# Block-causal attention with routed experts on one core: routing tables moved into PSUM, 64-byte list entries, a stacked tail product, and SP's queue in program order

## The chip, the cores and the metric

The kernel runs on one core of a Trainium2 chip. The metric is the device time in microseconds of one execution. The core has five engines that work through their own queues in order: PE (TensorE, matrix products; its weight loads are shown as PEld), DVE (VectorE), ACT (ScalarE), POOL (GpSimd) and SP (SyncE, which here only issues DMAs). POOL issues DMAs too, the indirect ones among them.

## The reference

What is computed, cut to its core:

```
scores = q @ k.T / 8                      # 8 batches x 8 heads, 576 positions, 64 channels
scores = where(i // 64 >= j // 64, scores, -1e9)
attn   = softmax(scores)                  # fp32, sums guarded by 1e-9
x      = (attn @ v) as rows of 512        # 4608 rows, 8 heads side by side
logits = x @ w_gate + modality_bias[modality_id]      # 8 experts
e      = argmax(logits);  gate = softmax(logits)[e]
out    = gate * (relu(x @ w1[e]) @ w2[e])             # w1: 512 x 1024, w2: 1024 x 512
```

The products must hold fp32 accuracy. The kernel gets it from products in fp32r by splitting operands into a head (the value rounded to fp32r) and a low half (value minus head) and adding head x head, head x low and low x head.

## The kernel before, in words

**Pairs and slots.** The 64 heads are taken in 32 pairs; four pairs make a batch of 576 rows. The program is written as slots. Slot s works on the front of pair s (stage 0) and on the back of pair s-1 (stage 1). What every engine does in a slot, and in which order, is one hand-written list, ORDER (L48): "SA2" are the scores of head A, row block 2; "M" the row maxima on DVE (L261); "E" the exponentials on ACT (L287); "T" the transposes on PE (L313 to L327); "C" the copies of transposed probabilities to SBUF as heads on ACT (L338); "D" their low halves on DVE (L343); "X", "Y", "W" the products with v (L380); "x", "y" the copies of their results on ACT; "K" the product that turns the result back into rows and adds the gate's columns (L399, L401); "Z" the scaling into the rows xr and the gate's sums gl on DVE (L412 to L415). "r" and "p" are the sums and reciprocals of a pair (L349 to L356). FIRST and LAST are the lists of the first and the last slot.

**Splitting q and k (split_qk, L194).** Once a slot, for the pair that follows, POOL casts the raw k (L198), subtracts to get k's low half on partitions 0 to 63 (L199), casts the raw q (L201) and subtracts to get q's low half (L202). q's raw tile holds the same 64 rows twice, so that q's head stands on partitions 0 to 63 and the low half, L202, on 64 to 127. SP copies k's low half (k2t, L192) and q's head (L204, into z) to where the second score product reads them, and loads the next q into the only raw tile (L184). Then POOL splits v (L233).

**The tail.** A head has 576 = 4 x 128 + 64 rows. Probabilities of the last 64 columns are transposed beside "TA1" (L321) and copied to a tile p4 in fp32 (L338); the product with v's last 64 rows is one fp32 product on 64 partitions at the end of "Y" (L378, L380).

**Routing.** Behind the last "Z" of a batch, routing(b) (L420) gives 24 small steps, which the places "q0" to "q7" in ORDER take one at a time (two at a time behind slot 24), and "qp", "qv" the steps for PE and what follows them. They form logits from gl (L429), treat the late 64 rows apart (L434 to L446), add the bias (L449), find the largest and the expert's number (L453 to L476), the gate's weight (L493 to L505), counts per expert by two small products (L481, L482), running sums (L500), and each row's place in its expert's list (L516 to L531). All these tables are SBUF tiles; the small products use the one bank of pool ps_b, which "K" also uses. With the weight, weight_out stores the batch's rows to DRAM (xrows, rows of 513 floats: 512 and the weight; L507 to L512, on SP). place_out appends five list writes to `placing`: indirect DMAs on POOL (L533), each of which writes 128 row numbers, four bytes each, to their places in idlist in DRAM. "vh" issues two of them per slot, behind v's split.

**SP's order.** For the first four slots (NSP, L39) SP's DMAs are issued in the order of the program; from then on a planner places them, by its own costs and due times. The four compute engines keep the program's order throughout.

**Experts.** Behind batch 5, `choose` (L565) picks the two largest experts and their first rows, weights are staged and cast during the last slots, and run_all (L934) works through tiles of 256 gathered rows: gather (L833), transposes (L846), two products (L864, L910), and an indirect store of the output rows (L913). fill (L624) sets idlist to a number that the gathers skip, before the first list write.

Of the kernel before, what the change touches and what calls it, by code (L numbers as in the profile page):

```python
# [25 lines left out]
PPB = H // 2  # L26
XW = 513
# [11 lines left out]
NSP = 4  # L39
# [52 lines left out]
def attention_moe(ctx, tc, qk, vr, bkw, mid, mb, w1, w2, cf, ci, cm, ld, out):  # L92
# [6 lines left out]
    idlist = drm.tile([NROW, 1], I32, name="idlist")  # L99
# [10 lines left out]
    idt = cst.tile([128, B, 5], I32, name="idt")  # L110
# [23 lines left out]

    q2s, k2s, zs, pts = [], [], [], []
# [17 lines left out]
    xrb = [rt.tile([128, 4, XW], F32, name=f"xr{i}", bufs=1) for i in range(2)]  # L153
    scatters, placing = [], []
# [39 lines left out]
    def split_qk(p):  # L194
        d = pairs[p]
        k = d.raw[0:64, 0:1152].rearrange("p (h c) -> p h c", h=2)
        q = rawq[64:128].rearrange("p (h c) -> p h c", h=2)
        pool.tensor_copy(d.qk[:, 1280:2560], d.raw)  # L198
        pool.tensor_tensor(d.k2[0:64], k, d.k[0:64], ALU.subtract)  # L199
        gather_low(d)  # L200
        pool.tensor_copy(d.qk[:, 0:1280], rawq)  # L201
        pool.tensor_tensor(d.q[64:128], q, d.q[64:128], ALU.subtract)  # L202
        if p > 2:
            nc.sync.dma_start(d.q2[0:64].bitcast(F32), d.q[0:64, :, 0:512].bitcast(F32))  # L204
        load_q(p + 1)

    def split_half(p, h):
# [7 lines left out]
        (dve, pool)[p * h].tensor_tensor(d.q[64:128, h], rawq[64:128, qs], d.q[64:128, h], ALU.subtract)  # L215
        act.copy(d.q2[0:64, h], d.q[0:64, h, 0:512])
# [6 lines left out]
    def load_v(p):  # L223
        d = pairs[p]
        d.vr = att.tile([128, 640], F32, name="vrt", bufs=3)
        nc.sync.dma_start(d.vr, vr[p])
        d.v = att.tile([128, 8, 2, 64], F32R, name="vhl", bufs=2)

    def split_v(p):
        d = pairs[p]  # L230
        v8 = d.vr[:, 0:512].rearrange("p (a b) -> p a b", a=8)
        act.copy(d.v[:, :, 0], v8)
        pool.tensor_tensor(d.v[:, :, 1], v8, d.v[:, :, 0], ALU.subtract)  # L233
# [58 lines left out]
    def transposes(p, u):  # L292
# [23 lines left out]
        elif u[1] == "1":  # L316
# [23 lines left out]
    def rests(p, u):  # L340
        for s, dst in pairs[p].copies[u]:
            if len(dst) > 1:
                dve.tensor_tensor(dst[1], s, dst[0], ALU.subtract)  # L343
# [14 lines left out]
    def values(p, h, part):  # L358
        d = pairs[p]
        if part == "X":  # L360
            d.o[h, 0] = ps_o.tile([128, 512], F32, name="o0")
# [32 lines left out]
    def back(p, h):  # L394
        d = pairs[p]
        d.b[h] = ps_b.tile([128, 512], F32, name="b")
# [23 lines left out]
    def routing(b):  # L420
        xr, xt, gl = xrs[b]
        g = Pair()

# [3 lines left out]
        def logits():  # L427
            g.lg = t([128, 5, NE], name="lg")
            dve.tensor_reduce(g.lg[:, 0:4], gl, AX.X, ALU.add)  # L429

        def late_logits():
            g.lt = t([128, 2, NE], name="lt")
            lt = xt.rearrange("p q c -> p c q")
            dve.tensor_reduce(g.lt[:, 0], lt[:, 0:8], AX.X, ALU.add)  # L434
            dve.tensor_reduce(g.lt[:, 1], lt[:, 72:80], AX.X, ALU.add)

        def late_half():
            dve.tensor_tensor(g.lt, g.lt, hm.unsqueeze(2).to_broadcast([128, 2, NE]), ALU.mult)
            dve.tensor_tensor(g.lt[:, 0], g.lt[:, 0], g.lt[:, 1], ALU.add)

        def late_total():
            g.tot = ps_b.tile([128, 512], F32, name="b")
            pe.matmul(g.tot[:, 0:NE], ii, g.lt[:, 0], start=True, stop=True)

        def late_copy():
            dve.tensor_copy(g.lg[:, 4, :], g.tot[:, 0:NE])  # L446

        def biased():
            dve.tensor_tensor(g.lg, g.lg, bias[:, 5 * b : 5 * b + 5, :], ALU.add)  # L449

        def top():
            g.mx = t([128, 5], name="mx")
            dve.tensor_reduce(g.mx, g.lg, AX.X, ALU.max)  # L453

        def shifted():
            g.df = t([128, 5, NE], name="df")
            dve.tensor_tensor(g.df, g.lg, bc(g.mx), ALU.subtract)
# [5 lines left out]
        def hits():  # L463
            g.eq = t([128, 5, NE], name="eq")
            dve.tensor_tensor(g.eq, g.lg, bc(g.mx), ALU.is_equal)

        def hit_index():
            dve.tensor_tensor(g.eq, g.eq, iom40, ALU.mult)

        def first():  # L470
            g.ix = t([128, 5], name="ix")
            dve.tensor_reduce(g.ix, g.eq, AX.X, ALU.min)

        def onehot():
            g.oh = t([128, 5, NE], BF16, name="oh")
            dve.tensor_tensor(g.oh, iov40, bc(g.ix), ALU.is_equal)  # L476

        def counts():
            g.ps = ps_b.tile([128, 512], F32, name="b")
            ohe = g.oh.rearrange("p c e -> p (c e)")  # L480
            pe.matmul(g.ps[:, 0:40].rearrange("p (e c) -> p c e", e=NE), ones, ohe.rearrange("p (c e) -> p c e", e=NE), start=True, stop=True)  # L481
            pe.matmul(g.ps[:, 40:80], lead, ohe, start=True, stop=True)  # L482
# [6 lines left out]
        late_copy.kind = counts_copy.kind = "qv"

        def weight():
            g.sm = t([128, 5], name="gs")
            dve.tensor_reduce(g.sm, g.ex, AX.X, ALU.add)  # L493

        def weight_guard():
            dve.tensor_scalar(g.sm, g.sm, GUARD, None, ALU.add)

        def running():
            g.cum = t([128, NE, 5], name="cum")
            dve.tensor_tensor_scan(g.cum.rearrange("p e c -> p (e c)"), first5.rearrange("p e c -> p (e c)"), g.pc[:, 0:40], 0.0, ALU.mult, ALU.add)  # L500

        def weight_out():
            g.wt = t([128, 1], name="wt")
            dve.reciprocal(xr[:, :, 512], g.sm[:, 0:4])
            dve.reciprocal(g.wt, g.sm[:, 4:5])  # L505
# [6 lines left out]
            queue.dma_start(late[:, 512:513], g.wt[64:128])  # L512

        def place():
            g.pos = t([128, 5, NE], name="pos")
            dve.tensor_tensor(g.pos, g.pc[:, 40:80].rearrange("p (c e) -> p c e", c=5), g.cum.rearrange("p e c -> p c e"), ALU.add)  # L516

        def place_run():
            dve.tensor_tensor(g.pos, g.pos, run.unsqueeze(1).to_broadcast([128, 5, NE]), ALU.add)

        def place_pick():
            dve.tensor_tensor(g.pos, g.pos, g.oh, ALU.mult)
            dve.tensor_tensor(run, run, g.cum[:, :, 4], ALU.add)

        def place_sum():
            g.pp = t([128, 5], name="pp")
            dve.tensor_reduce(g.pp, g.pos, AX.X, ALU.add)

        def place_out():
            g.pi = t([128, 5], I32, name="pi")  # L530
            dve.tensor_tensor(g.pi, g.pp, inv5, ALU.add)  # L531
            def scatter(c):
                last = pool.indirect_dma_start(idlist[:], bass.IndirectOffsetOnAxis(ap=g.pi[:, c : c + 1], axis=0), idt[:, b, c : c + 1], None, bounds_check=NROW - 1, oob_is_err=False)  # L533
# [6 lines left out]
        return [logits, late_logits, late_half, late_total, late_copy, biased, top, shifted, hits, expo, hit_index, first, onehot, weight, weight_guard, weight_out, counts, counts_copy, running, place, place_run, place_pick, place_sum, place_out]  # L540
# [3 lines left out]
    def pick(eng, val, name):  # L544
        mx = cst.tile([128, 1], F32, name=f"mx_{name}")
        kx = cst.tile([128, NE], F32, name=f"kx_{name}")
# [6 lines left out]
        eng.tensor_scalar(oh, iom8, ix, None, ALU.is_equal)  # L553
# [10 lines left out]

    def choose(eng):  # L565
        cnt, cnb, lead, rest, start = (cst.tile([128, NE], F32, name=n) for n in ("cnt", "cnb", "taken", "rest", "start"))
        eng.tensor_tensor(cnt, run, base8, ALU.subtract)
        sel["oha"], sel["ea"] = pick(eng, cnt, "a")
# [3 lines left out]
        sel["ohb"], sel["eb"] = pick(eng, cnb, "b")  # L572
        eng.tensor_tensor(rest, base8, lead, ALU.add)
        sel["ra"] = dot(eng, oha, base8, "a")
        sel["rr"] = dot(eng, oha, rest, "r")
        sel["rb"] = dot(eng, sel["ohb"], base8, "b")
        eng.scalar_tensor_tensor(start, oha, float(COVER - LEAD), rest, ALU.mult, ALU.add)
        eng.scalar_tensor_tensor(start, sel["ohb"], float(COVER_B), start, ALU.mult, ALU.add)
# [55 lines left out]
    def prepare_bias(dst, r):  # L634
# [10 lines left out]
        prepare_fill,  # L645
    ]

# [430 lines left out]
```

## Time and profile before

| what | value |
|---|---|
| median of three timed runs | 934.86 us (934.0 to 944.07) |
| the profiled execution's own time | 926.34 us |
| its span, first to last instruction | 924.2 us |
| mean granted TensorE clock | 0.962 |
| PE busy | 862.1 us, 93% |
| DVE busy | 506.8 us, 55% |
| ACT busy | 456.3 us, 49% |
| POOL busy | 442.8 us, 48% |
| DMA moved | 116.44 MB, mean 126 GB/s |

All profile numbers come from one execution. A line of a group gives the line of the code, the engine, the operation, out<-in by the names of the tiles, shapes, how often; then busy us, the mean ns of one, and the engine's idle time just ahead of them with what ended it. A line of the timeline gives start and duration in us and, in brackets, the idle time ahead of it and its releaser. The releaser of a wait for several semaphores is the one that came last by the profile. Busy shares are averages over stages with different limits; the attention with its routing runs to about 480 us, the experts from there to the end.

### The profile page before, as it was taken

Reading aid. Unit: us, or ns where it says so; the run is one execution under the profiler, and the core shown is the slowest. Engines: PE = TensorE matmul, PEld = TensorE weight load, DVE = VectorE, ACT = ScalarE, POOL = GpSimd, SP = SyncE. Lnnn points to the kernel's source line nnn. Section 1 sums busy time; section 2 is a strip of 40 time slices with the busy share of each in tenths; the row PEclk is TensorE's granted clock in tenths of the full one; section 3 lists DMA queues with packets and bytes.
Section 4 is the critical chain, followed back from the end, with each engine's and each line's share of the span. In section 5 each row is a group of like instructions: output and inputs, shape, how many; then the busy total and the mean of one; then the engine's idle time right before and its main releaser. Section 6 shows DMA issues by size and latency. Waiting matters only on the chain. (4 is left out here: it accounts for less than half of the span.)

```text
span 924.2 us, 16600 instructions
## 1 busy us (share of the span) xinstructions
PE 862.1 (93%) x5816; PEld 782.5 (85%) x5816; DVE 506.8 (55%) x1657; ACT 456.3 (49%) x1368; POOL 442.8 (48%) x300
## 2 busy tenths in 40 slices
PE   6999989998988978979989999999999999999996
PEld 4889978897877967868879989999999999999985
DVE  6789979999988966998964111111112222222220
ACT  6788858787876865857842222222222222222221
POOL 1977657778766677757574452222221111111100
PEclk7899979999998988999999999999999999999998
DMA  6766745757648576674796032211122222221100
GB/s 174 231 191 187 222 118 180 215 148 212 186 118 215 135 146 190 186 148 133 157 286 198 2 126 69 69 68 68 68 69 69 70 68 68 68 68 35 38 23 16
DMA packets 54308, 116.44 MB, mean 126 GB/s; under 512 B 12194, under 2 KB 20786, under 8 KB 54216
## 3 DMA queue, kind: packets, MB, share of 16 engines
q1 hardware_dynamic: 43520, 92.13, 36.5%
q0 software_dynamic: 10704, 23.24, 7.8%
q8 instruction: 47, 0.77, 0.4%
q14 instruction: 37, 0.30, 0.2%
HBM read 79.53 MB, written 19.33 MB: 107 GB/s over the span
## 5 line engine op out<-in xcount | busy, mean ns | idle before, releaser
L287 ACT ACTIVATE pm<-s,nm 128x256 f32<-128x256 f32 (+3 forms) x256 | 134.9, 532 | 53.6 <-DVE scratch L261 49.7
L343 DVE TENSOR_TENSOR ptl<-t,pth 128x512 fp32r<-128x512 f32 (+3 forms) x288 | 139.3, 502 | 18.6 <-ACT pth L338 17.4
L338 ACT CAST pth<-t 128x512 fp32r<-128x512 f32 (+3 forms) x288 | 123.2, 457 | 53.1 <-PE t L313 37.7
L261 DVE TENSOR_SCALAR_CACHE_REDUCE scratch<-s 128x128 bf16<-128x128 f32 (+4 forms) x288 | 130.9, 478 | 22.2 <-PE s L257 17.5
L380 PE MATMUL o<-pth,vhl 128*128 128x256 f32 (+1 forms) x384 | 119.8, 328 | 0.6 <-POOL vhl L233 0.6
L871 DVE SCALAR_TENSOR_TENSOR qkt<-s,qkt 128x512 fp32r<-128x512 f32 x18 | 12.4, 688 | 192.3 <-ACT qkt L870 192.3
L202 POOL TENSOR_TENSOR qkt<-rawq,qkt 64x1280 fp32r<-64x1280 f32 x30 | 87.6, 2920 | 53.7 <-DMA idlist<-idt,pi 21.9
L380 PE MATMUL o<-ptl,vhl 128*128 128x256 f32 (+1 forms) x384 | 112.6, 305 | 0.0
L912 ACT ACTIVATE scratch<-o,gw 128x512 f32<-128x512 f32 x37 | 25.5, 688 | 172.4 <-PE o L910 96.5
L199 POOL TENSOR_TENSOR z<-raw,qkt 64x1152 fp32r<-64x1152 f32 x30 | 79.4, 2647 | 49.5 <-issue 37.2
L256 PE MATMUL s<-qkt 128*128 128x256 f32 (+2 forms) x256 | 93.5, 375 | 7.0 <-POOL qkt L202 4.1
L913 POOL DMA_INDIRECT out<-scratch,ids_b x17 | 17.0, 1001 | 162.5 <-ACT scratch L912 156.6
L257 PE MATMUL s<-z 68*128 68x256 f32 (+2 forms) x256 | 83.5, 341 | 9.0 <-DMA z<-qkt 9.0
L864 PE MATMUL s<-z,w0hb 128*128 128x256 f32 x512 | 91.2, 281 | 0.0
L864 PE MATMUL s<-z,qkt 128*128 128x256 f32 x720 | 89.9, 283 | 0.0
L864 PEld LDWEIGHTS s<-z,qkt 128*128 128x128 f32 x720 | 88.4, 192 | 0.7
L864 PEld LDWEIGHTS s<-z,w0hb 128*128 128x128 f32 x512 | 79.1, 188 | 0.6
L380 PEld LDWEIGHTS o<-pth,vhl 128*128 128x128 f32 x384 | 76.7, 200 | 2.5 <-POOL vhl L233 1.0
L380 PEld LDWEIGHTS o<-ptl,vhl 128*128 128x128 f32 x384 | 77.0, 201 | 1.4
L864 PE MATMUL s<-z,w0lb 128*128 128x256 f32 x256 | 71.9, 281 | 0.0
L399 PE MATMUL b<-bk,ot 128*128 128x72 f32 x512 | 66.0, 273 | 0.0
L399 PEld LDWEIGHTS b<-bk,ot 128*128 128x128 f32 x512 | 65.7, 196 | 0.0
(227 smaller groups left out, 2001.6 us busy)
## 6 DMA issues: line engine op xcount, KB each, us to landing
raw<-qk SPq DMA_DIRECT2D x30, 640.0 KB
rawq<-qk SPq DMA_DIRECT2D x30, 640.0 KB
raw<-w SPq DMA_DIRECT2D x23, 512.0 KB
vrt<-vr SPq DMA_DIRECT2D x32, 320.0 KB
k2t<-z SPq DMA_DIRECT2D x64, 144.0 KB
xrows<-xr SPq DMA_DIRECT2D x8, 1026.0 KB
z<-qkt SPq DMA_DIRECT2D x29, 256.0 KB
qkt<-w POOLq DMA_DIRECT2D x3, 512.0 KB, 8.8
```

The lines of the kernel that those rows point to most:

```text
L199: pool.tensor_tensor(d.k2[0:64], k, d.k[0:64], ALU.subtract)
L202: pool.tensor_tensor(d.q[64:128], q, d.q[64:128], ALU.subtract)
L256: pe.matmul(o, d.q[:, h, qs], d.k[:, h, 0:n], start=True, stop=False)
L257: pe.matmul(o, d.q2[0:68, h, qs], d.k2[0:68, h, 0:n], start=False, stop=True)
L261: dve.tensor_scalar(jks[jturn[0] % 4][:, 0 : s.shape[-1]], s, -SCALE, start, ALU.mult, ALU.min, accum_out=o)
L287: act.activation(d.pm[h][:, CHUNK_OFF[c] : CHUNK_OFF[c] + n], s[:, 256 * i : 256 * i + n], AF.Exp, bias=d.nm[:, h, c : c + 1], scale=SCALE ...
L338: act.copy(dst[0], s)
L343: dve.tensor_tensor(dst[1], s, dst[0], ALU.subtract)
L380: pe.matmul(o, w, r, start=part != "W" and i == 0, stop=part != "Y" and i == len(mm) - 1)
L399: pe.matmul(d.b[h][:, 72 * c : 72 * c + 72], d.ot[h][:, 128 * c : 128 * c + 128], w, start=True, stop=True)
L864: nc.tensor.matmul(hp[:, a, :], w[:, kc, ms], x[:, kc, :], start=i == 0, stop=i == len(mm) - 1)
L912: nc.scalar.mul(yo, y, s.gw[:, i : i + 1])
```

## The change

- **q's halves change places.** L202's subtraction now works on partitions 0 to 63, and q's head is copied from partitions 64 to 127. The copy of the head stands ahead of the subtraction, and the load of the next q moves from split_qk to "q4".
- **Tail.** p4 becomes an fp32r tile of 128 partitions: the head on 0 to 63, and on 64 to 127 the low half, which DVE makes and a DMA (SP; ACT in the last two pairs) moves there. v's tail is split like the rest of v (ten blocks in place of eight), its 64 rows standing twice. One fp32r product with the stacked probabilities takes the place of the fp32 product, and stands inside "W".
- **Tables in PSUM.** The banks of o0 (X's output, which uses columns 0 to 255) and of ps_b become fixed tiles. Nearly all routing tables move to columns 256 to 511 of o0's bank (for the last batch, to ps_b's), as do the two small products; the copies of counts to SBUF go. `choose` keeps its tables in ps_b's bank from column 368 on. late_half is written as two operations with pointer scalars.
- **Lists.** An entry of idlist is 16 words (64 bytes), all the same number; the numbers to write are loaded per batch. The fill writes eight pieces, spread over steps. Rows of xrows have 528 floats. "vh" issues one list write per slot (two in the first slot of a batch and behind slot 24), and three places "+place" are added to the last slot.
- **SP.** All of SP's DMAs of the attention stay in the program's order. The row stores become a step of their own, one place behind weight_out, at "q7", and "q7" moves behind "MA01"; so they are issued behind the slot's copies of k2t and of q's head.

```
-XW = 513
+XW = 528
+IW = 16
...
-    ("SA2", 0), ("CA2", 1), ("vh", 0), ("MA2", 0), ("SA01", 0), ("TB0", 1), ("q7", 2), ("CB0", 1),
-    ("XA", 1), ("DA2", 1), ("EA2", 0), ("St0", 0), ("MA01", 0), ("Mt0", 0), ("EA01", 0), ("YA", 1),
+    ("SA2", 0), ("CA2", 1), ("vh", 0), ("MA2", 0), ("SA01", 0), ("TB0", 1), ("CB0", 1),
+    ("XA", 1), ("DA2", 1), ("EA2", 0), ("St0", 0), ("MA01", 0), ("q7", 2), ("Mt0", 0), ("EA01", 0), ("YA", 1),
...
-        q = rawq[64:128].rearrange("p (h c) -> p h c", h=2)
+        q = rawq[0:64].rearrange("p (h c) -> p h c", h=2)
...
         pool.tensor_copy(d.qk[:, 0:1280], rawq)
-        pool.tensor_tensor(d.q[64:128], q, d.q[64:128], ALU.subtract)
-        if p > 2:
-            nc.sync.dma_start(d.q2[0:64].bitcast(F32), d.q[0:64, :, 0:512].bitcast(F32))
-        load_q(p + 1)
+        nc.sync.dma_start(d.q2[0:64].bitcast(F32), d.q[64:128, :, 0:512].bitcast(F32))
+        pool.tensor_tensor(d.q[0:64], q, d.q[0:64], ALU.subtract)
...
-        v8 = d.vr[:, 0:512].rearrange("p (a b) -> p a b", a=8)
-        act.copy(d.v[:, :, 0], v8)
-        pool.tensor_tensor(d.v[:, :, 1], v8, d.v[:, :, 0], ALU.subtract)
+        v = d.vr.rearrange("p (a b) -> p a b", a=10)
+        act.copy(d.v[:, :, 0], v)
+        pool.tensor_tensor(d.v[:, :, 1], v, d.v[:, :, 0], ALU.subtract)
...
+        if u == "A1":
+            d = pairs[p]
+            (nc.sync if p < NPAIR - 2 else act).dma_start(d.p4[64:128].bitcast(F32), d.p4l.bitcast(F32))
...
-            last = (d.o[h, 1][0:64, 256:320], d.vr[0:64, 512 + 64 * h : 576 + 64 * h], d.p4[:, 64 * h : 64 * h + 64])
-            mm = mm[0:4] + [last] if part == "Y" else mm[6:8] + mm[4:6]
+            last = (d.o[h, 1][:, 256:320], d.v[:, 8 + h].rearrange("p a b -> p (a b)"), d.p4[:, 64 * h : 64 * h + 64])
+            mm = mm[0:4] if part == "Y" else mm[6:8] + [mm[4], last, mm[5]]
...
+        bank = bbank if b == B - 1 else o0[:, 256:512]
+        lt = bank[:, 0:16].rearrange("p (a e) -> p a e", a=2)
+        tot = bank[:, 16:24]
+        lg = bank[:, 24:64].rearrange("p (c e) -> p c e", c=5)
+        eq = bank[:, 64:104].rearrange("p (c e) -> p c e", c=5)
+        ps = bank[:, 104:184]
+        cum = bank[:, 184:224].rearrange("p (e c) -> p e c", e=NE)
+        ix, pp, sm = bank[:, 224:229], bank[:, 232:237], bank[:, 240:245]
...
-            dve.tensor_tensor(g.pos, g.pc[:, 40:80].rearrange("p (c e) -> p c e", c=5), g.cum.rearrange("p e c -> p c e"), ALU.add)
+            dve.tensor_tensor(g.pos, ps[:, 40:80].rearrange("p (c e) -> p c e", c=5), run.unsqueeze(1).to_broadcast([128, 5, NE]), ALU.add)
...
-            dve.tensor_tensor(g.pos, g.pos, run.unsqueeze(1).to_broadcast([128, 5, NE]), ALU.add)
+            dve.tensor_tensor(eq, cum.rearrange("p e c -> p c e"), g.pos, ALU.add)
...
+        def stores():
             queue = nc.sync
             queue.dma_start(xrows[S * b : S * b + 512, :].rearrange("(c p) w -> p c w", p=128), xr)
...
+            g.idt = t([128, 5, IW], I32, name="idt")
+            queue.dma_start(g.idt, ci[b].rearrange("p (c w) -> p c w", c=5))
...
-                last = pool.indirect_dma_start(idlist[:], bass.IndirectOffsetOnAxis(ap=g.pi[:, c : c + 1], axis=0), idt[:, b, c : c + 1], None, bounds_check=NROW - 1, oob_is_err=False)
+                last = pool.indirect_dma_start(idlist[:], bass.IndirectOffsetOnAxis(ap=g.pi[:, c : c + 1], axis=0), g.idt[:, c, :], None, bounds_check=NROW - 1, oob_is_err=False)
...
+            if name == "q4" and 0 < slot < NPAIR - 1:
+                load_q(slot + 2)
...
-                for _ in range(2):
-                    if placing and slot < NPAIR - 1:
+                for _ in range(2 if slot % PPB == 0 or slot > EARLY * PPB else 1):
+                    if placing and slot < NPAIR:
...
-        for slot in range(NSP):
+        for slot in range(NPAIR + lag):
             run_slot(slot)
     with tc.manual_schedule(engines=engines):
-        for slot in range(NSP, NPAIR + lag):
-            run_slot(slot)
```

More of the change, by code (lines that the diff above doesn't have):

```diff
@@ L98, in attention_moe @@
     xrows = drm.tile([N, XW], F32, name="xrows")
-    idlist = drm.tile([NROW, 1], I32, name="idlist")
+    idlist = drm.tile([NROW, IW], I32, name="idlist")
     cft = cst.tile([128, cf.shape[1]], F32, name="cf")
@@ L360, in values @@
         if part == "X":
-            d.o[h, 0] = ps_o.tile([128, 512], F32, name="o0")
+            d.o[h, 0] = o0
         if part == "Y":
@@ L474, in onehot @@
         def onehot():
             g.oh = t([128, 5, NE], BF16, name="oh")
[L476 removed]
+            dve.tensor_tensor(g.oh, iov40, bc(ix), ALU.is_equal)
         def counts():
[L479 removed]
             ohe = g.oh.rearrange("p c e -> p (c e)")
[L481 to L482 removed]
@@ L484, in counts_copy @@
-        def counts_copy():
-            g.pc = t([128, 80], name="pc")
-            dve.tensor_copy(g.pc, g.ps[:, 0:80])
-        late_total.kind = counts.kind = "qp"
[L489 to L500, printed above, removed]
+            pe.matmul(ps[:, 0:40].rearrange("p (e c) -> p c e", e=NE), ones, ohe.rearrange("p (c e) -> p c e", e=NE), start=True, stop=True)
@@ new lines, in counts, with weight, weight_guard, running @@
+            pe.matmul(ps[:, 40:80], lead, ohe, start=True, stop=True)
+        def weight():
+            dve.tensor_reduce(sm, g.ex, AX.X, ALU.add)
+        def weight_guard():
+            dve.tensor_scalar(sm, sm, GUARD, None, ALU.add)
+        def running():
+            dve.tensor_tensor_scan(cum.rearrange("p e c -> p (e c)"), first5.rearrange("p e c -> p (e c)"), ps[:, 0:40], 0.0, ALU.mult, ALU.add)
+        late_total.kind = counts.kind = "qp"
+        late_copy.kind = running.kind = "qv"
@@ L563, in dot @@
         return i
+    ranks, bases, cnt, cnb, kx, rest, begin = (bbank[:, 368 + NE * i : 368 + NE * i + NE] for i in range(7))
     def choose(eng):
-        cnt, cnb, lead, rest, start = (cst.tile([128, NE], F32, name=n) for n in ("cnt", "cnb", "taken", "rest", "start"))
-        eng.tensor_tensor(cnt, run, base8, ALU.subtract)
-        sel["oha"], sel["ea"] = pick(eng, cnt, "a")
+        lead, start = (cst.tile([128, NE], F32, name=n) for n in ("taken", "start"))
+        eng.tensor_tensor(cnt, run, bases, ALU.subtract)
+        sel["oha"], sel["ea"] = pick(eng, cnt, "a", kx, ranks)
         oha = sel["oha"]
@@ L644, in attention_moe @@
         lambda: dve.tensor_tensor(bias, bias, btmp, ALU.add),
-        prepare_fill,
-    ]
+        lambda: dve.tensor_copy(ranks, iom8),
+        lambda: dve.tensor_copy(bases, base8),
+        lambda: dve.memset(fill, int(BIG)),
+    ]
+    for i in range(IW // 2):
+        steps += [lambda i=i: prepare_fill(i)] + [lambda: None] * (0 < i < 6)
     def run_slot(slot):
@@ L659, in run_slot @@
                 if ex is None:
-                    ex = Experts(ctx, tc, cst, scratch, btmp, con["edges"], xrows, idlist, idf, w1, w2, out, sel, run, base8, pick, dot, ps_s, ps_t, ps_o, placing, qkts, raws, zs, pts, xrb)
+                    ex = Experts(ctx, tc, cst, scratch, btmp, con["edges"], xrows, idlist, idf, w1, w2, out, sel, run, base8, pick, dot, ps_s, ps_t, ps_o, o0, placing, qkts, raws, zs, pts, xrb)
                 ex.early(what)
@@ L684, in run_slot @@
             emit(name, p)
-            if slot == 1 and name in ("xB", "yB"):
-                h = "xy".index(name[0])
-                act.copy(pairs[2].q2[0:64, h], pairs[2].q[0:64, h, 0:512])
             if name == "vh":
-                for _ in range(2):
-                    if placing and slot < NPAIR - 1:
+                for _ in range(2 if slot % PPB == 0 or slot > EARLY * PPB else 1):
+                    if placing and slot < NPAIR:
                         g, c = placing.pop(0)
@@ L702, in attention_moe @@
         load(0)
-        warm = ps_b.tile([128, 512], F32, name="b")
         for _ in range(NWARM):
-            pe.matmul(warm, ones, jks[0], start=True, stop=True)
+            pe.matmul(bbank, ones, jks[0], start=True, stop=True)
         nc.sync.dma_start(cft, cf)
@@ L719, with __init__ @@
 class Experts:
-    def __init__(self, ctx, tc, cst, scratch, btmp, edges, xrows, idlist, idf, w1, w2, out, sel, run, base8, pick, dot, ps_s, ps_t, ps_o, placing, qkts, raws, zs, pts, xrb):
+    def __init__(self, ctx, tc, cst, scratch, btmp, edges, xrows, idlist, idf, w1, w2, out, sel, run, base8, pick, dot, ps_s, ps_t, ps_o, o0, placing, qkts, raws, zs, pts, xrb):
         self.__dict__.update(locals())
@@ L770, in early @@
             self.up_products(self.parts[0], int(what[2]))
+        elif what == "place":
+            if self.placing:
+                g, c = self.placing.pop(0)
+                g(c)
         elif what == "relu":
```

111 lines of the change are left out of this document (54 added, 57 removed), and 4 rows, old and new, of the table LAST.

## The prediction

> **What bounds the kernel now.** I first cut the span into stages of four pairs each, at the start of the sums L349 (once per slot), and read the table of busy time by window: window, its length, then busy us (and instructions) of PE, PEld, DVE, ACT and POOL, then the granted clock, the DMA engines' busy share and GB/s.
>
> ```profile
> 79.76:137.58 57.82, 53.76 (x379) 49.88 (x377) 50.93 (x183) 43.50 (x151) 36.97 (x21) 0.91 0.61 174
> 137.58:190.92 53.34, 49.91 (x379) 45.79 (x378) 50.67 (x183) 43.07 (x151) 42.34 (x26) 1.00 0.66 189
> 190.92:246.56 55.64, 51.21 (x379) 47.16 (x378) 52.52 (x183) 43.18 (x151) 42.17 (x26) 0.97 0.64 180
> 246.56:305.83 59.27, 53.02 (x379) 48.57 (x378) 52.38 (x182) 43.29 (x151) 42.07 (x26) 0.94 0.65 170
> 305.83:368.98 63.15, 53.31 (x384) 49.03 (x382) 46.88 (x184) 43.31 (x151) 43.46 (x26) 0.89 0.67 163
> 368.98:398.08 29.10, 25.35 (x192) 23.12 (x190) 27.66 (x101) 21.73 (x77) 20.45 (x14) 1.00 0.77 169
> 398.08:480.22 82.14, 70.64 (x505) 64.90 (x504) 69.25 (x240) 54.13 (x187) 55.89 (x38) 0.94 0.69 176
> 480.22:924.20 443.98, 433.92 (x2792) 392.87 (x2790) 95.25 (x192) 103.42 (x169) 110.29 (x95) 0.99 0.22 70
> ```
>
> Behind 480.22 (the experts) PE is busy 433.92 of 443.98 us at 0.99 of its clock: nothing in the change shortens that work. The attention, with the routing between its pairs, is another matter. The 22 slots from 79.76 to 398.08 take 57.82 + 53.34 + 55.64 + 59.27 + 63.15 + 29.10 = 318.3 us, 14.5 each. Single slots do better:
>
> ```profile
> 55.57:67.39 11.82, 11.82 (x93) 11.07 (x92) 9.93 (x40) 10.62 (x39) 9.02 (x6) 1.00 0.88 284
> 179.40:190.92 11.52, 11.52 (x89) 10.68 (x89) 10.55 (x46) 10.62 (x39) 8.10 (x6) 1.00 0.55 170
> ```
>
> Here PE is busy all the time at full clock; 11.7 us is what PE needs for a pair. So 2.8 us of the average slot are stalls and the low clock that follows them. The waits and POOL's timeline tell where they come from.
>
> ```profile
> POOL qkt L202 <- DMA idlist<-idt,pi: 21.9, 8, 6.4
> PE t L318 <- DVE ptl L343: 23.2, 22, 3.4
> PE s L257 <- DMA z<-qkt: 9.0, 4, 4.9
> ```
>
> ```profile
> 323.72 2.91 POOL L202 TENSOR_TENSOR qkt<-rawq,qkt 64x1280 fp32r<-64x1280 f32 x1 [6.36 <-DMA idlist<-idt,pi]
> 326.71 1.28 POOL L233 TENSOR_TENSOR vhl<-vrt,vhl 128x512 fp32r<-128x512 f32 x1
> 328.14 1.01 POOL L533 DMA_INDIRECT idlist<-idt,pi  x1 [0.15 <-PE s L257]
> 329.46 0.97 POOL L533 DMA_INDIRECT idlist<-idt,pi  x1 [0.31 <-issue]
> 331.78 2.63 POOL L199 TENSOR_TENSOR z<-raw,qkt 64x1152 fp32r<-64x1152 f32 x1
> 340.90 2.88 POOL L202 TENSOR_TENSOR qkt<-rawq,qkt 64x1280 fp32r<-64x1280 f32 x1 [5.28 <-DMA k2t<-z]
> ```
>
> L202, the low half of the next pair's q, begins 10.5 us behind the end of the last list write's issue (329.46 + 0.97), though nothing that it reads comes from one; the median list write takes 9.7 us to land (below), so I read the label of the second wait, k2t, as the same wait. L199, the same operation on partitions 0 to 63, began 1.4 us behind that issue and did not wait. So the wait belongs to L202 alone, the Pool subtraction that starts at partition 64. From one L202 to the next that is 340.90 - 323.72 = 17.2 us: the slots with two list writes cannot be shorter.
>
> ```profile
> 336.27 0.52 SPq L512 DMA_DIRECT2D xrows<-wt  x1
> 336.90 1.32 SPq L204 DMA_DIRECT2D z<-qkt  x1
> 343.83 0.69 PE L256 MATMUL s<-qkt 128*128 128x384 f32 x1 [4.10 <-POOL qkt L202]
> 349.42 0.69 PE L257 MATMUL s<-z 68*128 68x384 f32 x1 [4.90 <-DMA z<-qkt]
> ```
>
> In that slot PE pays: it waits 4.10 us for L202 and 4.90 us for the copy of q's head, issued directly behind the row stores on SP's queue (336.27, 336.90) and landed 12 us later. The third cost is DVE, 88 to 95% busy in the stages up to 246.56. Its groups by form (busy, mean ns of one):
>
> ```profile
> L519 DVE TENSOR_TENSOR pos<-pos,run 128x40 f32<-128x40 f32 x8 | 8.5, 1062 | 0.0
> L438 DVE TENSOR_TENSOR lt<-lt,cf 128x16 f32<-128x16 f32 x8 | 8.4, 1048 | 0.1
> L457 DVE TENSOR_TENSOR df<-lg,mx 128x40 f32<-128x40 f32 x8 | 7.6, 954 | 0.0
> L413 DVE TENSOR_TENSOR gl<-b,rc 128x32 f32<-128x32 f32 x64 | 13.3, 207 | 0.0
> ```
>
> Sixteen or forty elements cost 954 to 1062 ns where both inputs lie in SBUF; thirty-two cost 207 ns where one comes from PSUM. [...]
>
> **The change, part by part.** (1) *Low half of q on partitions 0 to 63.* The wait before L202 goes. PE, DVE and POOL loops are then limited by work, not by a landing. POOL's work per slot:
>
> ```profile
> L202 POOL TENSOR_TENSOR qkt<-rawq,qkt 64x1280 fp32r<-64x1280 f32 x30 | 87.6, 2920 | 53.7 <-DMA idlist<-idt,pi 21.9 <-DMA k2t<-z 10.6 <-DMA xrows<-wt 7.0
> L199 POOL TENSOR_TENSOR z<-raw,qkt 64x1152 fp32r<-64x1152 f32 x30 | 79.4, 2647 | 49.5 <-issue 37.2 <-DMA raw<-qk 7.2 <-POOL qkt L198 2.3
> L233 POOL TENSOR_TENSOR vhl<-vrt,vhl 128x512 fp32r<-128x512 f32 x32 | 40.9, 1278 | 2.4
> L533 POOL DMA_INDIRECT idlist<-idt,pi x40 | 39.6, 991 | 10.2 <-issue 7.7 <-DMA idlist<-idt,pi 0.8 <-PE t L299 0.5
> L198 POOL CAST qkt<-raw 128x1280 fp32r<-128x1280 f32 x30 | 38.0, 1266 | 2.5 <-DMA raw<-qk 2.4
> L201 POOL CAST qkt<-rawq 128x1280 fp32r<-128x1280 f32 x30 | 37.4, 1246 | 0.6 <-DMA rawq<-qk 0.6
> ```
>
> 2.92 + 2.65 + 1.27 + 1.25 + 1.28 x 10/8 (v's split now takes ten blocks) + 5/4 list writes x (0.99 + 0.31 issue) = 11.3 us, about 11.6 with the gaps between them. That is what is late next: POOL, at the pace of PE.
>
> (2) *Tail product in fp32r on 128 partitions.* Now it is two passes of 64x64 with a change of mode around them:
>
> ```profile
> 189.75 0.31 PE L380 MATMUL o<-pth,vhl 128*128 128x320 f32 x1
> 189.90 0.31 PE L380 MATMUL o<-ptl,vhl 128*128 128x320 f32 x1
> 190.13 0.32 PE L380 MATMUL o<-p,vrt 64*64 64x64 f32 x2
> 190.39 0.55 PE L318 MATMUL t<-cf,pm 128*128 128x128 f32 x3
> ```
>
> From the last 320-column product to the transpose 0.49 us, of which 0.15 is that product's own step: 0.34 for the tail. One fp32r product of 64 columns is in no row; it costs between nothing and the 0.15 of a 320-column one, and I take 0.11. Two per pair: 0.46 less, and PE needs 11.2 us. The price is one small subtraction on DVE (0.2, next to L413), a quarter more of v's cast on ACT (busy 10.6 of 11.5 to 11.8, so hidden) and a 32 KB copy on SP at the end of each slot, behind which the next raw loads queue; those are needed a slot later.
>
> (3) *Tables in PSUM.* The rows above are the dearest of thirteen two-SBUF steps a batch (L438 to L531); at 0.8 us on average (an estimate below those rows) against L413's 0.2 that is 13 x 0.6 = 8 us of DVE time a batch, 2 a slot. DVE goes from 52.5 / 4 = 13.1 to 11.3 us a slot: off the path in the slots up to 398, and itself the path just behind them:
>
> ```profile
> 398.08:415.32 17.24, 12.59 (x91) 11.45 (x90) 17.07 (x59) 10.40 (x39) 11.26 (x7) 0.94 0.61 162
> ```
>
> There the choice of experts and doubled routing steps fill DVE for 17.07 of 17.24 us; they fall most. [...]
>
> (4) *SP in program order, stores behind the heads.* The five stores and loads of a batch (0.5 us of issue each) now come behind k2t and the head of q, and ahead of the next rawq load, which waits for POOL anyway. The copies no longer stand behind 1 MB of stores: the 9.0 us of PE's waits above go. The moved step q7 is one DVE instruction, now behind the maxima, so that X's first product need not wait for it.
>
> (5) *64-byte entries.* Landing now and, as the nearest larger row, of whole output rows:
>
> ```profile
> idlist<-idt,pi POOLq DMA_INDIRECT x40, 9.7
> out<-scratch,ids_lead POOLq DMA_INDIRECT x6, 3.0
> ```
>
> Between 3.0 and 9.7 us (a little over, if something is worse); I take 6. With (1) no engine waits for it in the attention; the last ones are waited for by POOL's loads of the lists behind the attention, under PE's work for the experts. [...] Rows of 528 words make stores and gathers 3% larger; the stores are now behind what the next scores need, the gathers under PE's 433.92 us of the experts, and without that cover a gather would cost its 3% of some 4 us. One list write per slot in place of two, and the three in the last slot, are counted in POOL's 5/4. The fill grows from 0.15 to 2.5 MB in slots 2 to 4, where the DMA share is 0.88 in the row of 55.57: 0 to 6 us late, I take 1.
>
> **The sum.** Slots 79.76 to 398.08: the larger of PE 11.2 and POOL 11.6, and 0.5 for waits between them, 12.1 x 22 = 266, against 318: -52. The five slots to 480.22: DVE's 8 us of choice and tables and the tail products, -10 (bounds -3 to -20). Slots before 79.76: -2 for tails, +1 for the fill. Experts: 0. In all -63. The profiled execution took 926.3 us (span 924.2); it becomes 863. The median of the three shown is 934.9, 8.5 above it, so I predict 934.9 - 63 = 872.
>
> **Rivals.** *A, half of it.* The tables share a PSUM bank with X's output, and POOL runs at its own limit; slots stop at 13.3. For it: the 23.2 us in which PE waits for DVE's L343 are not touched by name. Against: DVE gets 2 us per slot. 22 x 1.2 = 26 us less gain, 4 less behind: about 902. *B, PE alone limits.* POOL's list writes slip into idle time, slots at 11.3: 18 more, and 5 more behind: 849. Against: POOL's sum of 11.3 without a gap. *C, slower.* Each of X's products (two a slot) must now wait until DVE's last table step in that bank is done, and DVE is in order: PE hangs on DVE's backlog, which the waits show up to 3.4 us (L318 <- L343). At 2 us for each of 2 x 28, 112 us are lost against 63 won: 934.9 + 49 = 984. It decides from 63 / 56 = 1.1 us per wait. Against: the last step before each X stands about as far ahead of it as two groups of transposes, 1 us, and DVE's steps shrink to a quarter. [...] *D, nothing.* PE's rate decides whatever POOL and DVE do, and the low clock stays: within 1%. Against: the 11.52 us slot.
>
> **Chances.** Forecast (slots near 12.1) 0.58, A 0.22, B 0.11, C 0.06, D 0.03. Faster by over 1% (about what a measurement of this kernel tells from no change) 0.91, within 0.03, slower 0.06. The range reaches from B to A with the fill's bound: 845 to 905, leaving C, D and the edges out.
>
> **What would show it.** Right: no idle time before Pool's q subtraction by a list write; the table operations at 0.1 to 0.3 us; the tail product once per head, with no 64x64 rows; the stages of four slots at 46 to 50 us, clock 1.00, POOL 45 or more busy; no wait of scores for z. Wrong: X's products or their weight loads waiting for DVE's table rows; slots over 13 with POOL idle; list writes still in front of a Pool instruction; loads of rawq late behind the stores.

## The result and the profile after

The changed kernel takes 857.25 us (median of four runs, 856.16 to 858.68) beside 935.14 for the kernel before on the same chip (median of four, 934.00 to 944.07): a ratio of 0.915, 95% interval 0.91 to 0.92. That lies in the predicted range, 15 us below the predicted 872. The profiled execution took 856.18 us, its span 854.5.

The same table by window as for the kernel before, cut again at the start of the sums (now L353): window, length, busy us (and instructions) of PE, PEld, DVE, ACT, POOL, then granted clock, DMA share, GB/s.

```profile
79.55:126.26 46.71, 46.71 (x370) 45.56 (x369) 42.64 (x186) 43.48 (x150) 38.77 (x21) 1.00 0.73 218
126.26:172.96 46.70, 46.70 (x370) 45.56 (x369) 42.63 (x185) 43.49 (x150) 41.94 (x25) 1.00 0.76 222
172.96:219.66 46.70, 46.70 (x370) 45.57 (x369) 42.62 (x185) 43.48 (x150) 43.32 (x26) 1.00 0.75 220
219.66:266.44 46.78, 46.78 (x371) 45.65 (x370) 42.70 (x185) 43.55 (x150) 42.91 (x26) 1.00 0.75 221
266.44:313.60 47.16, 47.16 (x372) 46.00 (x372) 43.09 (x188) 43.95 (x151) 44.19 (x27) 1.00 0.75 222
313.60:337.14 23.54, 23.52 (x184) 22.38 (x182) 22.62 (x104) 21.49 (x75) 21.92 (x14) 1.00 0.80 235
337.14:407.54 70.40, 65.83 (x496) 62.55 (x495) 57.80 (x243) 54.76 (x185) 60.36 (x41) 0.98 0.72 203
407.54:854.50 446.96, 433.81 (x2791) 392.90 (x2789) 98.24 (x191) 103.19 (x169) 111.33 (x94) 0.99 0.22 72
```

PE is busy for all of the first six rows, at full clock. The 22 slots take 337.14 - 79.55 = 257.6 us, 11.71 each, where they took 318.3; POOL has about 0.8 us to spare in each (44.19 of 47.16 us at most). The five slots behind them take 70.4 for 82.1, the experts 447.0 for 444.0, everything ahead 79.55 for 79.76. That is -60.73 - 11.74 + 2.98 - 0.21 = -69.70 us.

The waits of the changed kernel: which engine and line, what it waited for, us in total, times, longest.

```profile
POOL z L202 <- issue: 18.0, 10, 3.6
POOL qkt L204 <- DMA rawq<-qk: 5.5, 7, 1.3
DVE oh L484 <- ACT ot L393: 3.8, 5, 0.8
PE s L257 <- DVE qkt L217: 3.4, 2, 2.6
PE t L319 <- DVE ptl L344: 1.9, 2, 1.7
```

No line has a wait for a list write in front of q's subtraction (21.9 us before), none has scores waiting for z (9.0), and PE's wait for DVE's low parts has shrunk from 23.2 to 1.9 us. The third row has no counterpart in before: DVE waits for ACT to read X's output from the bank that now holds the tables, 3.8 us in all.

DVE's routing groups by form (busy, mean ns of one):

```profile
L521 DVE TENSOR_TENSOR pos<-o,run 128x40 f32<-128x40 f32 x7 | 1.4, 199 | 0.2
L450 DVE SCALAR_TENSOR_TENSOR l<-o,cf,l 128x8 f32<-128x8 f32 x7 | 1.6, 226 | 0.2
L467 DVE TENSOR_TENSOR df<-o,mx 128x40 f32<-128x40 f32 x7 | 1.3, 180 | 0.0
L417 DVE TENSOR_TENSOR gl<-b,rc 128x32 f32<-128x32 f32 x64 | 13.2, 206 | 0.0
```

What took 954 to 1062 ns takes 180 to 226. And the tail in PE's timeline (start, us, line):

```profile
42.12 0.31 PE L384 MATMUL o<-pth,vhl 128*128 128x320 f32 x1
42.27 0.19 PE L384 MATMUL o<-p,vhl 128*128 128x64 f32 x1
42.30 0.39 PE L384 MATMUL o<-ptl,vhl 128*128 128x320 f32 x1
42.53 0.39 PE L257 MATMUL s<-qkt 128*128 128x512 f32 x1
```

The stacked product steps 0.03 us (42.27 to 42.30), but the 320-column product behind it then steps 0.23 (42.30 to 42.53) where the one ahead stepped 0.15 (42.12 to 42.27). So the tail costs 0.11 us a head; the medians over all 64 heads are the same to within 0.01.

Two of the kernels below (halves alone on the kernel before, and tables back in SBUF) vary from 932 to 958 and from 925 to 957 us, and their profiles, 956.3 and 955.6 us of span, are of slow executions, so their times are given for the fast runs and their rows show only where time went in those executions. Ratios are against runs of the kernel before on the chip of the same experiment (929 to 934 us there). Times of different experiments can come from different chips, and a difference of a few us between them shows nothing.

### The profile page after: what moved, and what is told of

Same layout as the page of the kernel before. It is cut to its first block, busy times and chain, and to the rows that moved or that the text cites. A ratio compares the mean times of both kernels' runs of the same rounds, so it can differ in the third digit from the quotient of the medians.

```text
span 854.5 us, 16606 instructions
## 1 busy us (share of the span) xinstructions
PE 825.8 (97%) x5752; PEld 767.1 (90%) x5752; DVE 455.5 (53%) x1685; ACT 457.7 (54%) x1366; POOL 454.6 (53%) x300
## 5 line engine op out<-in xcount | busy, mean ns | idle before, releaser
L384 PE MATMUL o<-pth,vhl 128*128 128x256 f32 (+1 forms) x384 | 115.5, 319 | 1.1 <-POOL vhl L234 0.9
L384 PE MATMUL o<-ptl,vhl 128*128 128x256 f32 (+1 forms) x384 | 115.6, 311 | 0.0
L257 PE MATMUL s<-qkt 128*128 128x256 f32 (+2 forms) x256 | 90.1, 362 | 3.4 <-DVE qkt L217 3.4
L202 POOL TENSOR_TENSOR z<-raw,qkt 64x1152 fp32r<-64x1152 f32 x30 | 79.6, 2654 | 22.2 <-issue 18.0
L258 PE MATMUL s<-z 68*128 68x256 f32 (+2 forms) x256 | 81.1, 332 | 0.0
L384 PEld LDWEIGHTS o<-pth,vhl 128*128 128x128 f32 x384 | 73.4, 191 | 4.3 <-POOL vhl L234 1.3
L384 PEld LDWEIGHTS o<-ptl,vhl 128*128 128x128 f32 x384 | 73.6, 192 | 1.4
```

The source lines that it names most:

```text
L257: pe.matmul(o, d.q[:, h, qs], d.k[:, h, 0:n], start=True, stop=False)
L258: pe.matmul(o, d.q2[0:68, h, qs], d.k2[0:68, h, 0:n], start=False, stop=True)
L384: pe.matmul(o, w, r, start=part != "W" and i == 0, stop=part != "Y" and i == len(mm) - 1)
```

## The experiments

**Undo one part at a time.** Theory L was that of the prediction: landings (the list writes in front of q's subtraction, z in front of the scores) were the stall. Its rival, T: the table steps on SBUF were. The first kernel moves q's low half back:

```
-        q = rawq[0:64].rearrange("p (h c) -> p h c", h=2)
+        q = rawq[64:128].rearrange("p (h c) -> p h c", h=2)
...
-        pool.tensor_tensor(d.q[0:64], q, d.q[0:64], ALU.subtract)
+        pool.tensor_tensor(d.q[64:128], q, d.q[64:128], ALU.subtract)
```

> The changed kernel with q's low half back on partitions 64 to 127, all else as changed. Theory L (landings): what held the slots of before was Pool's wait for the landing of the list writes, and PE's for z; with those gone PE alone sets 11.7 us a slot. By it the wait in front of q's subtraction comes back. Between a list write and that subtraction lie 1.25 + 2.65 + 1.25 = 5.2 us of Pool's work; if 64-byte entries land in 6 us as I took, Pool waits 1 to 1.5 us a slot and a slot is 10.75 + 1.3 = 12.1: 857 + 9 = 866 us. If they land as slowly as the 4-byte ones (9.7), Pool waits 4.5 a slot: 857 + 75 = 932. Theory T (tables): the slow two-input steps of DVE on SBUF tables, and Pool's work that they hold up, were the stall: 857, within 3.

856.3 us, ratio 0.922 (0.918 to 0.927): nothing lost, against the 866 or 932 of L. POOL's timeline of this run:

```profile
205.59 1.01 POOL L537 DMA_INDIRECT idlist<-idt,pi  x1
...
212.10 1.26 POOL L204 CAST qkt<-rawq 128x1280 fp32r<-128x1280 f32 x1 [1.37 <-DMA rawq<-qk]
213.44 2.92 POOL L206 TENSOR_TENSOR qkt<-rawq,qkt 64x1280 fp32r<-64x1280 f32 x1
```

The subtraction on partitions 64 to 127 follows the cast (ended 213.36) without a wait, 6.8 us behind the end of the list write's issue: a 64-byte write has landed by then (2.9 us is the median of this run). So the wait is gone without the move. The next kernel also takes the entries back to 4 bytes (`IW = 16` to `IW = 1`; the fill is one piece again):

> As the run before, and the list entries back to 4 bytes (one fill of 152 KB). Theory L: landing 9.7 us, so each list write, now one per slot, holds Pool 4.5 us: a slot near 15, in all 857 + 75 = 932, and the difference to the run before is what 64-byte entries bring. If both runs wait alike, the entry's size does nothing for the landing. Theory T: 857, within 3.

950.6 us, ratio 1.027 (1.020 to 1.034): slower than either theory had it. The write lands in 9.4 us again, and POOL's wait is back:

```profile
POOL qkt L207 <- DMA idlist<-idt,pi: 26.9, 10, 4.1
```

And the entries alone, with q's low half left where the change put it:

> The changed kernel with 4-byte list entries alone (q's low half stays on partitions 0 to 63). After four runs: undoing the halves alone cost nothing, halves and entries together 94 us on the chip of before's 929. If the only path of a late landing is Pool's wait before the subtraction on partitions 64 to 127, this run is the changed kernel's 857, within 5. If the small entries also hold up the other transfers (rawq, the tails), it is 10 to 60 slower.

951.7 us, ratio 1.017 (1.010 to 1.025): as slow, and outside what was expected, with no wait for a list write in front of q's subtraction at all. So with 4-byte entries the move does remove POOL's wait, and wins nothing by it. What stalls is in the waits and the table by window of this run:

```profile
PE o L385 <- DMA p<-p4l: 54.0, 19, 9.2
```

```profile
181.80:188.30 6.50, 2.89 (x20) 2.65 (x20) 3.64 (x20) 2.32 (x9) 6.42 (x3) 0.90 1.07 43
```

The window lies right behind two list writes (their issue ended at 179.0 and 180.2). The DMA share is 1.07 at only 43 GB/s. The packets in it are the load's own, 54 pieces of 5120 bytes with a median of 1.5 us; the list writes' small packets, ahead of the window, took about 0.01 us each. The changed kernel at the same place, behind its list writes of 166.9 and 168.2:

```profile
168.40:174.90 6.50, 6.50 (x55) 6.37 (x53) 6.43 (x32) 6.20 (x23) 6.33 (x4) 1.00 0.63 199
```

In the records of single packets the input loads' 5120-byte pieces take 0.2 to 0.3 us as a rule; between 60 and 560 us, 505 packets of 2 KB to under 8 KB took over 1.2 us in this run with 4-byte entries, up to 7.2, in clusters that mostly begin 2 to 7 us behind a list write; with 64-byte entries 23, up to 1.5; in the kernel before 155, up to 3.5. So the list writes with 4-byte entries hold up other transfers; here those are the loads of rawq and raw, and the tails' copy among them on SP's queue. What in the DMA engines does it, no run shows. How many bytes are enough (`IW = 16` to `IW = 8`):

> The changed kernel with 32-byte entries in place of 64. 4 bytes cost 95 us, 64 nothing that the trace shows. If anything below 64 bytes holds up the packets that follow, 900 to 952; if 32 are enough, 857 within 5; if the cost falls with the number of small writes per byte, half of it would not do, and it lies between.

856.6 us, ratio 0.922 (0.918 to 0.925), and 27 slow packets: 32 bytes do as well as 64.

Next, the tables back in SBUF, all else as changed:

```
+        tab = sml.tile([128, 256], F32, name="tab", bufs=2)
-        lg = bank[:, 24:64].rearrange("p (c e) -> p c e", c=5)
+        lg = tab[:, 24:64].rearrange("p (c e) -> p c e", c=5)
... (lt, eq, cum, ix, pp, sm and the tables of the choice likewise)
```

> The changed kernel with the routing tables and the tables of the choice in SBUF; only what TensorE writes stays in PSUM. Theory L: DVE does 10 two-SBUF steps a batch at some 0.8 in place of 0.2 us, 1.5 us a slot on top of the 10.7 it is busy: 12.2, so at most 0.5 us a slot in 22 slots and 5 us behind: 857 + 5 to 16 = 862 to 873. Theory T: the slots go back to 14.5 us: 857 + 60 = 917.

925.0 us in the lowest of four runs, 943 to 957 in the others, beside 929 for the kernel before here: above the 862 to 873 of L and the 917 of T, and hardly a gain. In the profiled execution, of 957 us, the slots take 15.7 us, for 14.5 in before. The groups, and a stretch of the timeline of both engines:

```profile
L475 DVE TENSOR_TENSOR tab<-tab,mx 128x40 f32<-128x40 f32 x5 | 15.0, 3005 | 0.0
L525 DVE TENSOR_TENSOR tab<-tab,pos 128x40 f32<-128x40 f32 x5 | 13.1, 2610 | 0.0
```

```profile
212.82 2.92 POOL L206 TENSOR_TENSOR qkt<-rawq,qkt 64x1280 fp32r<-64x1280 f32 x1
...
213.09 2.72 DVE L475 TENSOR_TENSOR tab<-tab,mx 128x40 f32<-128x40 f32 x1
215.70 1.54 POOL L234 TENSOR_TENSOR vhl<-vrt,vhl 128x640 fp32r<-128x640 f32 x1
215.73 0.45 DVE L262 TENSOR_SCALAR_CACHE_REDUCE scratch<-s 128x288 bf16<-128x288 f32 x1
```

Forty elements take DVE 2.72 us: the step starts 0.27 us into POOL's subtraction and ends 0.07 us behind it. By this row the price of such a step is what is left of POOL's instruction. The next kernel cuts POOL's five instructions into two or four each:

```
-        pool.tensor_tensor(d.q[0:64], q, d.q[0:64], ALU.subtract)
+        for a in range(4):
+            c = slice(320 * (a % 2), 320 * (a % 2) + 320)
+            pool.tensor_tensor(d.q[0:64, a // 2, c], q[:, a // 2, c], d.q[0:64, a // 2, c], ALU.subtract)
```

> The changed kernel with the tables in SBUF (944 us by itself) and each of Pool's five instructions of a pair cut into two or four of at most 0.8 us (the same work, some 1 us a slot more of fixed cost on Pool). Theory K (a two-input DVE step on SBUF waits for the end of Pool's current instruction, whatever its length): L475 falls from 3.0 us to 0.8 or less, the others likewise, and the time from 944 to 870 to 900. Rival (the two engines share a rate): the steps keep their 1 to 3 us and the time its 944, or more.

921.7 us, ratio 0.990 (0.986 to 0.993): outside the 870 to 900 of theory K, and only 3 us below the lowest run with whole instructions (925.0). That shorter instructions save time is not shown. Most steps are shorter than in the profile above, one is longer:

```profile
L458 DVE TENSOR_SCALAR l<-tab,cf 128x8 f32<-128x8 f32 x6 | 25.4, 4231 | 0.0
L483 DVE TENSOR_TENSOR tab<-tab,mx 128x40 f32<-128x40 f32 x6 | 9.2, 1528 | 0.0
L533 DVE TENSOR_TENSOR tab<-tab,pos 128x40 f32<-128x40 f32 x5 | 3.8, 762 | 0.0
```

```profile
192.33 5.23 DVE L458 TENSOR_SCALAR l<-tab,cf 128x8 f32<-128x8 f32 x1
192.58 3.31 POOL L212 TENSOR_TENSOR qkt<-rawq,qkt 64x320 fp32r<-64x320 f32 x4
195.87 1.66 POOL L242 TENSOR_TENSOR vhl<-vrt,vhl 128x320 fp32r<-128x320 f32 x2
197.60 0.29 DVE L459 SCALAR_TENSOR_TENSOR l<-tab,cf,l 128x8 f32<-128x8 f32 x1
```

L475 is L483 here: 3.0 to 1.5 us; L525 is L533: 2.6 to 0.76. But L458, which reads one table and a column of factors, begins before the train of six short instructions and ends with it, at 197.56: DVE did not get in between them. So "until POOL's current instruction ends" holds for part of the steps only; where POOL's instructions follow without a gap, a step can outlast several.

The order of SP's queue, back to the planner from slot 4 on:

```
+        for slot in range(NSP):
+            run_slot(slot)
+    with tc.manual_schedule(engines=engines):
+        for slot in range(NSP, NPAIR + lag):
-        for slot in range(NPAIR + lag):
             run_slot(slot)
-    with tc.manual_schedule(engines=engines):
```

> The changed kernel with SP's queue ordered by the planner from slot 4 on, as before. Theory L: in a slot with row stores z comes behind them, once in four slots, 2 to 5 us: 857 + 8 to 35, about 870, and the trace shows PE's L258 waiting for z. Theory T: 857, within 3.

876.1 us, ratio 0.946 (0.941 to 0.951): 19 us more, inside what L expected, but the wait is another one. z is not among PE's longer waits; the tails' copy, new with the change, is:

```profile
PE o L385 <- DMA p<-p4l: 11.4, 14, 2.0
```

The tail product back to two 64x64 passes, and v's split to eight blocks:

```
-            mm = mm[0:4] if part == "Y" else mm[6:8] + [mm[4], last, mm[5]]
+            mm = mm[0:4] + [last] if part == "Y" else mm[6:8] + mm[4:6]
```

> The changed kernel with the tail product back in fp32, 64x64, twice per head, and v's split back to 8 blocks. If PE alone limits the slots at 11.70 us, all of its extra time shows: by my term 0.46 us a pair x 28 = 13, by the count of instructions (before's slots had 94.75, its quoted best slot 89: 11.52 x 94.75 / 89 = 12.26 a slot) 0.56 x 28 = 16: 870 to 873. If Pool limits, as I forecast, this run is no slower than 857, and up to 0.3 us a slot faster.

865.8 us, ratio 0.927 (0.921 to 0.933). A stage of four slots of this run:

```profile
177.71:226.54 48.83, 48.83 (x379) 45.84 (x378) 42.54 (x181) 43.17 (x150) 42.15 (x26) 1.00 0.68 208
```

PE is busy throughout, 48.83 / 4 = 12.21 us a slot with the kernel before's 379 instructions: that is what PE needed per pair before the change. The stacked product brings 12.21 - 11.68 = 0.53 us a slot (46.70 / 4 in the changed kernel), though POOL has 0.3 us a slot more to do: PE limits, not POOL.

**One part alone, and two.** With L fallen (the halves cost nothing) and T not enough (4-byte entries cost 95 us with the tables in PSUM), the theory became C: each stall covers the other. By it SBUF is left to DVE while POOL stands idle for a landing; with the landings gone, DVE's table steps run into a busy POOL. Then no part alone brings much. First the halves, on the kernel before:

```
-        q = rawq[64:128].rearrange("p (h c) -> p h c", h=2)
+        q = rawq[0:64].rearrange("p (h c) -> p h c", h=2)
...
-        pool.tensor_tensor(d.q[64:128], q, d.q[64:128], ALU.subtract)
+        pool.tensor_tensor(d.q[0:64], q, d.q[0:64], ALU.subtract)
```

> The kernel before with q's low half moved to partitions 0 to 63, and nothing else (the copy of q's head for pair 2 goes to SP with the others). Theory L (each cost for itself): the 2.4 us a slot go, before - 50, ratio 0.945. Theory C (the stalls cover each other): in before Pool stands idle for the landing and leaves SBUF to DVE's table steps; with Pool always busy each of the two-input steps lasts until Pool's instruction ends, as where the tables alone were undone (1 to 3 us each, 944 us); so nothing is won: ratio 0.98 to 1.02.

932.3 to 945.4 us, ratio 1.007 (1.003 to 1.012): nothing won, a little lost, as C has it. The longest of PE's waits in the profiled execution (958.5 us), and a routing group:

```profile
PE t L317 <- DVE ptl L342: 48.9, 20, 6.2
```

```profile
L515 DVE TENSOR_TENSOR pos<-pc,cum 128x40 f32<-128x40 f32 x5 | 10.7, 2135 | 0.0
```

PE's wait on DVE is twice the 23.2 of before there; the other runs of this kernel have no profile, so this alone shows no cause. The other three kernels are the changed one with the edits above put together, and two list writes a slot in each (`range(2)`). They keep the rest of the change: the rows of 528 floats, the row stores as a step of their own, the later "q7" and load of q. "Alone" means: without the other parts that were undone above.

> The changed kernel with everything undone but the tables: q's low half on partitions 64 to 127, 4-byte entries, the planner's order on SP, the tail product in two 64x64 passes, two list writes a slot as before. Theory L: DVE gets 2 us a slot but Pool's wait stays: before - 10, ratio 0.99. If the tables are the main stall: ratio 0.94. Theory C says with L that the landing decides alone here: 0.98 to 1.02.

> The changed kernel with everything undone but the 64-byte entries: tables in SBUF, q's low half on partitions 64 to 127, the planner's order, the tail in two passes, two list writes a slot. Theory E (entries alone were the stall): before's slots lose 2.4 us, ratio 0.945. Theory C (each stall hides the other; both must go): as where the tables alone were undone, DVE's two-input steps each last until Pool's instruction ends, ratio 0.98 to 1.02.

> As the run before with the tables in PSUM as well: entries and tables, without the halves, SP's order and the tail. Tables alone gave 0.980, entries alone is the run before. If the two gains simply add and nothing else counts, 0.98 times that run's ratio. Theory C: only both together free the slots; 857 + 19 (SP's order, measured) + 9 (the tail, measured) = 885 us, ratio 0.95.

Tables alone: 914.8 us, ratio 0.980 (0.974 to 0.986), at the edge of what C said. Entries alone: 920.9, 0.989 (0.985 to 0.994). Both: 871.3, 0.938 (0.935 to 0.940), where the product of the two would be 0.969 and C had said 0.95. The 22 slots of the entries alone, then of both:

```profile
81.60:401.77 320.17, 289.24 (x2076) 266.14 (x2075) 295.51 (x1004) 239.66 (x822) 232.69 (x138) 0.95 0.60 179
```

```profile
79.71:348.69 268.98, 268.98 (x2074) 252.53 (x2073) 235.56 (x1004) 237.37 (x821) 228.66 (x135) 1.00 0.69 210
```

Entries alone leave the slots where they were (320.2 for 318.3 us; DVE busy 295.5 for 281.0). One table step, before and with the entries alone:

```profile
L465 DVE TENSOR_TENSOR eq<-lg,mx 128x40 f32<-128x40 f32 x6 | 5.3, 876 | 0.0
L473 DVE TENSOR_TENSOR tab<-tab,mx 128x40 f32<-128x40 f32 x6 | 14.8, 2468 | 0.0
```

In these slots PE's waits for POOL and for z, 4.1 and 9.0 us in before, are gone, and its waits for DVE have grown from 16.2 to 29.4 us. That is what theory C says. With the tables as well PE never stops: 268.98 / 22 = 12.23 us, PE's own time with the old tail.

The tables alone are another case. Their 22 slots, and the five behind them:

```profile
79.91:364.21 284.30, 275.47 (x2074) 257.32 (x2073) 236.22 (x1003) 237.90 (x821) 224.29 (x133) 0.98 0.67 191
364.21:459.08 94.87, 75.36 (x508) 69.29 (x507) 58.62 (x239) 55.02 (x185) 59.68 (x41) 0.87 0.67 161
```

In the 22 slots they bring 34 of the 49 us that both bring, though POOL still waits 21.2 us for list writes; there theory C does not hold for them. The five slots behind take 94.9 us for 82.1, which hides part of it in the total: PE waits there for z, for POOL's q subtraction and for gathered rows. With the entries as well those five take 76.1.

What is left, from 871.3 to 857.25, lies in tail, order, halves and the one list write a slot; only the halves were shown to cost nothing. With the planner's order the stacked tail seems to lose (ratio 0.938 without, 0.946 with it, where its copy comes late; the number of list writes differs too); with program order it wins (865.8 to 857.25).

## Why the prediction was right, and where its steps were not

The number was right in part by luck: steps (1) and (5) were wrong, and the slot time came out near for another reason than the one given. The sum of -63 us in the profile came out as -69.7; the other half of the 15 us between 872 and 857 is the median of before standing 8.8 us above its own profiled run, while that of the changed kernel stands 1.1 above.

- *What bounds it.* "11.7 us is what PE needs for a pair" was wrong by 0.5. The quoted slot of 11.52 us held 89 PE instructions, a stage of four holds 379, 94.75 a slot: 11.52 x 94.75 / 89 = 12.26, and 12.21 to 12.23 is what two runs measured. The cut at the sums does not fall at the same place of PE's work each time; the counts beside the times say so.
- *(1) Halves.* The step that failed. The wait was real, but in the changed kernel the shorter landing removes it, not the move (the halves undone: 856.3); with 4-byte entries the move does remove it and brings nothing (950.6 and 951.7 in the changed kernel, 1.007 on the kernel before). I had named L202 on partitions 64 to 127 as the cause and counted its wait as lost time; what DVE does while POOL waits was left out. Why a subtraction on those partitions waits for the list write, no run shows.
- *(5) Entries.* "I take 6. With (1) no engine waits for it in the attention" failed most: the landing itself is 2.9 us in place of 6, which mattered little, but in the changed kernel the entries are worth 95 us, and 44 us (914.8 to 871.3) where the old tail has no copy to wait for. I looked at who waits for the list write, not at what the list write holds up. 32 bytes landed in 3.1 us and 64 in 2.9, 4 bytes in 9.4 to 10.4.
- *(3) Tables.* The direction was right, the size came from a fixed price of 0.8 us a step. The price varies with what POOL does meanwhile: in before L516 and L519 took 0.22 and 0.19 us at 339.31 and 340.09, while POOL stood idle (335.62 to 340.90); L475 took 2.72 beside POOL's subtraction with the tables in SBUF. The mean of L465 is 0.88 us in before, 2.47 for the same step with the entries alone. POOL's subtractions fill 2.92 + 2.65 + 1.28 = 6.85 of 14.5 us in before, and nothing shows them held up in turn: q's takes 2.92 us there and 2.93 in the changed kernel. Without this part the change would bring next to nothing (925.0 in the lowest run, for 929).
- *(2) Tail.* 0.46 us a pair predicted, 0.53 measured in the slots; the new tail costs the 0.11 us a head that was taken.
- *(4) Order.* z's waits went, as said; but "copies behind the next raw loads, needed a slot later" missed that the new tails' copy is what the order now protects (19 us).
- *The larger of PE and POOL.* POOL was to limit at 11.6, and 45 us or more of a stage were to be busy; it is busy 38.8 to 44.2, at most 11.05 us a slot. My sum counted 5/4 list writes at 1.3 us, 0.3 of it idle time, where 24 fall into 22 slots. PE alone limits, which was rival B's mechanism; with PE's true 12.2 in place of 11.7 B's 11.3 becomes about the measured 11.7. That the forecast of 12.1 stood near is luck: POOL's 11.6, which limits nothing, happens to be close to PE's true need, and the 0.5 for waits, which did not come, made up the rest.
- *Rival C*, X's products waiting for table steps in their bank, did not happen: PE waits for none of them. Only two of back's products wait, 0.9 us each, for the tables of the choice that share their bank:

```profile
PE b L403 <- DVE b L88: 0.9, 1, 0.9
```

- *Five slots* -11.7 for -10, *slots ahead* -0.2 for -1. *Experts* +3.0 for 0: PE is busy the same 433.8 us, and idles 13.2 in place of 10.1.

## What to carry to other kernels

When two stalls stand side by side in a profile, ask what each engine does during the other's stall before pricing either: here tables and entries alone brought 2% and 1%, the halves nothing, and tables and entries together 6%. And look at each stretch by itself, since a loss in one can hide a gain in another, as with the tables alone. A transfer that nobody waits for still has a price if it holds up others, as the 4-byte list writes did (95 us): look at the DMA share and the GB/s in the microseconds behind it. And before a best slot is taken as an engine's need, compare its number of instructions with the mean.

## What the runs showed of the hardware

- Behind indirect writes of 4 bytes per row the 5120-byte packets of a load on another queue took up to 7.2 us, and for some 6 us they alone made up a DMA share of 1.07 at 43 GB/s; in the changed kernel, with 64 bytes or with 32, none took over 1.6 us. Why the kernel before, with the same 4 bytes, suffers less (155 slow packets for 505) was not tried; its list writes go out in twos and its loads stand elsewhere.
- A DVE step of 40 elements with both inputs in SBUF took 0.20 us while POOL stood idle (207.79 in the profile with the tables in SBUF, POOL idle from 206.29 to 208.89) and 2.5 us on average for the dearest line with the entries alone; one of 8 elements outlasted six POOL instructions in a row (5.23 us).
- The same addition, in PSUM and in SBUF (after, then the entries alone):

```profile
L459 DVE TENSOR_TENSOR o<-o,bias 128x40 f32<-128x40 f32 x6 | 1.2, 207 | 0.2
```

```profile
L458 DVE TENSOR_TENSOR tab<-tab,bias 128x40 f32<-128x40 f32 x6 | 1.2, 200 | 0.2
```

One source and the result in PSUM cost 7 ns here.
